# A second layer's in-projection in seven block products, with its weights split in advance

## The chip, the cores and the metric

One of the eight cores of one Trainium2 chip runs the kernel. The metric is the device time of one execution, in microseconds, as the median of repeated runs. The engines work side by side and each takes its instructions in the order of the program: TensorE (PE in the profile, its weight loads PEld), VectorE (DVE), ScalarE (ACT), GpSimd (POOL) and SyncE (SP), which issues nearly all DMAs.

## The reference

Attention inside chunks of 64 tokens, a gated layer, and a second layer with the activation h - tanh(h), for 8 x 576 = 4608 tokens of 512 features:

```
attn = softmax(q k^T / 8) v          per head and chunk of 64
x    = attn, as (4608, 512)
y    = (silu(x @ w_gate) * (x @ w_val)) @ w_out      w_gate, w_val: 512 x 1536
h    = y @ w2_in                                     w2_in: 512 x 2048
out  = (h - tanh(h)) @ w2_out                        w2_out: 2048 x 512
```

All weights come as 64-bit floats.

## The kernel before, in words

**Numbers.** Each float is split into a high and a low half that TensorE reads exactly; a product takes three passes (`PASSES`: high x high, high x low, low x high). Splitting is a cast to the high half (`copy`, L294, ACT) and a subtraction for the low one (`sub`, L252, DVE). A 64-bit weight is first turned into a float by `convert`: a load into a `raw` tile, one ACT instruction (`mag`) and four on DVE.

**Sweeps, blocks, units.** Tokens go in 9 blocks of 512. There are three sweeps over the blocks: sweep 0 and sweep 1 do half each of the gated layer's 1536 hidden features (3 pairs of 256 for each block), sweep 2 the second layer (8 pairs for each block). A *unit* is one block and one pair of two strips of 128 hidden features: 27 + 27 + 72 units. Between sweeps the activations go to DRAM and back (`xd`, `x2p`, `x2d`).

**The gated layer** (sweeps 0 and 1) multiplies in blocks. `x_set` makes four blocks and three sums of blocks of the activations (B11, B21, B22, T1 to T4) and splits them, `cols_set` does so for the weights, and `in_proj` then needs seven products (a to g, `ORDER`) in place of eight, each of 6 matmuls with 256 columns. The products share two PSUM banks, X for a, c, e, g and Y for b, d, f; between them ACT copies a partial sum out (`snap0` to `snap3`) or DVE adds one (L249).

**The second layer** (sweep 2) multiplies directly: `in_whole` makes each strip in four steps (one for each 128 input features) of three matmuls with 512 columns, into a bank for each strip. `cubic_set` computes h - tanh(h) from that bank: ACT makes the square, the tanh and a bracket (`sq`, `th`, `br`), DVE a comparison, h - tanh, a cube, a polynomial and a selection (`gt`, `re`, `cu`, `po`, `se`), then the split (`h`, `l`). All of its weights stay in SBUF.

**Out-projection.** `out_parts` of a unit are eight steps of three matmuls with 512 columns, worked off two units later. After the last pair of a block ACT or DVE copies the finished sums out.

**The order of the work** is written out by hand. `PE` has a letter for each step of a unit (letters or digits for the in-projection, `o` for a step of the out-projection). One letter is one *slot*. The table `AT` gives for every other step the slot after its start at which it is issued, `ON` the engine, `START` the start of each preparation of weights. What is issued on an engine runs in that order there.

**Weights of the second layer before.** During sweep 1 `ahead_set` converts them into a `cvt` tile and stores that to DRAM. `whole_set` loads the floats back around the start of sweep 2 and splits them into tiles that stay.

Of the kernel before, what the change touches and what calls it, by code (L numbers as in the profile page):

```python
# [1257 lines left out]
```

## Time and profile before

| | |
|---|---|
| median of 3 runs | 1842.05 us (1841.13 to 1843.69) |
| span of the profiled execution | 1838.3 us, 3.75 us below the median |
| TensorE busy in the span | 1754.7 us |
| VectorE, ScalarE, GpSimd busy | 1341.1, 923.3, 176.7 us |
| sweep 2's first and last in-projection matmul start | 1020.8 and 1821.8 us |

The profile is of one execution; its own time outside the span is not recorded, so the difference to the median is all that is known of it. Times in the rows are from the span's start. A busy PE says that matmuls follow one another, not at which rate; the rate is read from counts in a window.

### The profile page before, as it was taken

The numbers are of one execution on the slowest core, as the hardware profiler recorded it, in microseconds if no ns is written. First come the engines' busy times: TensorE is split into PE (matmuls) and PEld (weight loads), VectorE is DVE, ScalarE is ACT, GpSimd is POOL, SyncE is SP. The second block draws the span as 40 slices with busy tenths as digits, with TensorE's granted clock in tenths as the row PEclk, the third lists the DMA queues.
The fourth block names the chain that finished last, engine by engine and source line by source line (L and its number), as shares of the span: only waits on it lengthen the run. The fifth ranks groups of instructions, "written<-read, shape, count | busy, mean of one in ns | idle before, by whom it ended". The sixth has DMA issues, their size and how long they took to land.

```text
span 1838.3 us, 30622 instructions
## 1 busy us (share of the span) xinstructions
PE 1754.7 (95%) x11800; PEld 1509.2 (82%) x11800; DVE 1341.1 (73%) x2438; ACT 923.3 (50%) x1772; POOL 176.7 (10%) x251
## 2 busy tenths in 40 slices
PE   4679999999999899999999999999999999999999
PEld 3669888888898899999998888888888888888887
DVE  7897888778767777777755777676676767676765
ACT  4566655665555544444444545444444444444443
POOL 2233333333210000000000000000000000000000
PEclk9799999999999999999999999999999999999999
DMA  7545545555432454444424401010101000000000
GB/s 183 145 108 135 132 117 144 138 129 130 100 98 70 138 172 138 155 145 148 144 75 149 161 12 46 1 47 0 47 3 44 22 25 23 24 23 24 1 23 23
DMA packets 220802, 158.25 MB, mean 86 GB/s; under 512 B 155376, under 2 KB 180848, under 8 KB 218352
## 3 DMA queue, kind: packets, MB, share of 16 engines
q1 hardware_dynamic: 214256, 148.95, 28.1%
q0 software_dynamic: 6400, 7.35, 1.5%
q8 instruction: 92, 1.51, 0.3%
q14 instruction: 54, 0.44, 0.1%
HBM read 105.38 MB, written 50.86 MB: 85 GB/s over the span
## 4 chain that ended last, share of the span: by engine, by line
PE 85%; DVE 9%; DMA 2%; ACT 2%; issue 1%; SPq 0%; POOL 0%; DVEq 0%; ACTq 0%; POOLq 0%
PE acc L1058 35%; PE H L562 22%; PE Xg L508 7%; PE Xv L508 6%; PE Yg L508 6%; PE Yv L508 5%; PE ppt L671 1%; PE po L746 1%; PE sc L735 1%; DVE xb_B L296 1%; DMA f_wi<-cvt_wi 1%; DVE scratch L252 1%; DVE vs L249 0%; DVE mx L644 0%; DVE xb_B L252 0%
## 5 line engine op out<-in xcount | busy, mean ns | idle before, releaser
L562 PE MATMUL H<-xb,wi 128*128 128x512 f32 x1728 | 490.3, 394 | 0.0
L1058 PE MATMUL acc<-wp,h 128*128 128x512 f32 x1728 | 488.3, 394 | 0.0
L562 PEld LDWEIGHTS H<-xb,wi 128*128 128x128 f32 x1728 | 324.5, 188 | 77.0
L1058 PEld LDWEIGHTS acc<-wp,h 128*128 128x128 f32 x1728 | 324.7, 188 | 75.7
L1058 PE MATMUL acc<-h,wo 128*128 128x512 f32 x1296 | 364.0, 397 | 0.5 <-DVE wo L252 0.5
L1058 PEld LDWEIGHTS acc<-h,wo 128*128 128x128 f32 x1296 | 220.3, 189 | 29.2 <-DVE wo L252 1.0
L508 PEld LDWEIGHTS Xg<-xb_T,wg 128*128 128x128 f32 x972 | 138.5, 191 | 18.2 <-ACT s L294 2.5
L508 PE MATMUL Xg<-xb_T,wg 128*128 128x256 f32 x972 | 144.5, 285 | 3.1 <-DVE xb_T L252 1.7
L712 POOL DMA_DIRECT2D vr<-in_v_dram x200 | 115.8, 591 | 201.2 <-PE po L746 197.2
L294 ACT CAST h<-g 128x512 fp32r<-128x512 f32 x72 | 44.7, 620 | 166.3 <-DVE g L973 166.3
L294 ACT CAST h<-vr 128x512 fp32r<-128x512 f32 x72 | 44.7, 620 | 120.3 <-DVE vr L973 118.1
L508 PE MATMUL Yv<-xb_B,wv 128*128 128x256 f32 x648 | 96.4, 284 | 6.4 <-ACT s L294 4.6
L508 PE MATMUL Xv<-xb_T,wv 128*128 128x256 f32 x648 | 97.7, 287 | 4.1 <-ACT s L294 2.6
L252 DVE TENSOR_TENSOR h<-vs,h 128x512 fp32r<-128x512 f32 x108 | 75.0, 694 | 36.5 <-ACT h L294 35.6
L921 ACT ACTIVATE gs<-gs 128x512 f32<-128x512 f32 x108 | 68.4, 633 | 63.4 <-DVE gs L249 63.1
L508 PE MATMUL Yg<-xb_B,wg 128*128 128x256 f32 x648 | 96.2, 284 | 3.2 <-ACT vs L294 3.2
L508 PEld LDWEIGHTS Yg<-xb_B,wg 128*128 128x128 f32 x648 | 89.2, 191 | 8.5 <-ACT vs L294 3.4
L508 PEld LDWEIGHTS Yv<-xb_B,wv 128*128 128x128 f32 x648 | 84.8, 188 | 11.9 <-ACT s L294 8.2
L508 PEld LDWEIGHTS Xv<-xb_T,wv 128*128 128x128 f32 x648 | 84.7, 190 | 5.1 <-ACT s L294 2.8
L294 ACT CAST h<-vs 128x512 fp32r<-128x512 f32 x108 | 67.2, 623 | 42.3 <-DVE vs L255 21.6
L252 DVE TENSOR_TENSOR h<-g,h 128x512 fp32r<-128x512 f32 x72 | 49.9, 693 | 51.2 <-ACT h L294 51.2
L252 DVE TENSOR_TENSOR h<-vr,h 128x512 fp32r<-128x512 f32 x72 | 49.9, 692 | 46.3 <-ACT h L294 46.3
(235 smaller groups left out, 2744.1 us busy)
## 6 DMA issues: line engine op xcount, KB each, us to landing
xd<-xra SPq DMA_DIRECT2D x36, 256.0 KB, 2.9
x2p<-ob SPq DMA_DIRECT2D x36, 256.0 KB, 2.7
xr_xd<-xd SPq DMA_DIRECT2D x9, 1024.0 KB, 5.2
ob<-x2p SPq DMA_DIRECT2D x36, 256.0 KB, 4.4
x2d<-ob SPq DMA_DIRECT2D x36, 256.0 KB, 2.6
xr_x2d<-x2d SPq DMA_DIRECT2D x9, 1024.0 KB, 4.8
out_dram<-ob SPq DMA_DIRECT2D x36, 256.0 KB, 2.0
raw_wi<-in_moe_w_in_dram SPq DMA_DIRECT2D x16, 512.0 KB, 4.8
```

The costliest lines, as they stand in the source:

```text
L252: eng.tensor_tensor(out=out_, in0=a, in1=b, op=ALU.subtract)
L294: eng.copy(out_, in_)
L296: eng.tensor_copy(out_, in_)
L508: nc.tensor.matmul(bank, w[:, wl, kk * 128:(kk + 1) * 128], x[xn][:, xl, kk, :], start=start and n == 0, stop=n == 5, skip_group_check=not ...
L562: nc.tensor.matmul(u["ps"][j], w[:, wl, k * 128:(k + 1) * 128], x[k][:, xl], start=k == 0 and n == 0, stop=k == KC - 1 and n == 2,)
L671: nc.tensor.transpose(pt[:, m, :], z["p"][:, m].rearrange("p e j -> p (e j)"), ident)
L712: nc.gpsimd.dma_start(out=vr[p:p + C, n + skip:n + m:2], in_=chunks[:, skip:m:2],)
L735: nc.tensor.matmul(sc[e ^ c][c * C:(c + 1) * C, m, :], z["qT"][h, cut], z["kT"][h, cut], start=True, stop=True,)
L746: nc.tensor.matmul(po[c][h, m, :], z["vr"][f, 2 * m + c, :], z["pT"][f, m, c * C:(c + 1) * C], start=True, stop=True,)
L921: return lambda: nc.scalar.activation(out=gs[i], in_=gs[i], func=AF.Silu)
L1058: nc.tensor.matmul(u["acc"][d], l, r, start=p0 and i == 0 and n == 0, stop=p1 and i == 1 and n == 2,)
```

## The change

Three things change, all for the second layer.

1. Its in-projection goes through `in_proj`, as the gated layer's does: seven products a to g of 6 matmuls with 256 columns, so `x_set` now also makes the blocks and sums for sweep 2. A unit has 15 slots in place of 16. `cubic_set` reads the strips from SBUF (tiles `gs`), makes the comparison on ACT (a ReLU of the square minus the threshold) and works in place.
2. The weights are converted and split during sweep 1, one pair in each of the first eight blocks (`split_cols`, `split_rows`), and the split tiles are stored to DRAM. The in-weights are loaded once and stay (`fetch_cols`).
3. The out-weights don't stay: `stream` loads a tile of 512 KB for each strip of each unit, three tiles ahead, when the matmuls on an older tile have been issued.

`raw` tiles and split tiles come from the pool `wrp`, which has 10 buffers in place of 8.

```diff
-PE = ["abocdoefoogABCoDEoFGoo", "aAobBocCodDoeEofFogGoo", "0o1o2o3o4o5o6o7o"]
-LAST = "0o1o2o3o4567oooo"
+PE = ["abocdoefoogABCoDEoFGoo", "aAobBocCodDoeEofFogGoo", "aobocodoeofogoo"]
+LAST = "aobocodoeofogoo"
...
-    wrp = ctx.enter_context(tc.tile_pool(name="wrp", bufs=F2 // 2))
+    wrp = ctx.enter_context(tc.tile_pool(name="wrp", bufs=F1 // 2 + 4))
...
+    def split_rows(start, w, f, nm):
+        z = {}
+        step = Steps("dr", start, f"{nm}{f}")
+        convert(step, "", z, 0, f"{nm}{f}", tile_of(w, f, False), False)
+        def tile():
+            z["t"] = wrp.tile([128, 2, DM], F32R, tag="w", name=f"{nm}{f}")
+            return z["t"][:, 0], z["t"][:, 1]
+        def then():
+            nc.sync.dma_start(out=wf[nm, f], in_=z["t"].bitcast(F32))
+            done.add(("wf", nm, f))
+        halves(step, "", tile, lambda: z["c", 0], ["tl"], then)
...
+    def stream(u, i):
+        w = u["w"][i] = wrp.tile([128, 2, DM], F32R, tag="w", name=f"wp{u['nm']}_{i}")
+        nc.sync.dma_start(out=w.bitcast(F32), in_=wf["wp", 2 * u["pr"] + i])
...
+                if sw.kind == 2 and d == KC - 1 and u["next"][i]:
+                    stream(*u["next"][i])
...
             def large(z=z, tl=tl):
-                nc.vector.tensor_scalar(
-                    out=tl("m"), in0=z["u"], scalar1=SMALL * SMALL, scalar2=None, op0=ALU.is_gt
-                )
+                nc.scalar.activation(
+                    out=tl("m"), in_=z["u"], func=AF.Relu, bias=bias[:, 1:2]
+                )
...
+    for pr in range(h2):
+        first = base[n0[1] + h1 * pr]
+        slot = first + START["dc"]
+        sets.append((slot, lambda slot=slot, pr=pr: split_cols(slot, w2_in, pr, "wi")))
...
-                hp_ = in_whole(u, x)
-                pe = [hp_[int(j)] if j != "o" else j for j in form]
-                cubic_set(u, [b + form.index(j) + 1 for j in "37"])
+                odd = u["pr"] % 2
+                piece = dict(zip("abcdefg", in_proj(
+                    si, wcol["i"], u["pr"], x, lazy("gs", odd),
+                    ("a0", "a1") if odd else ("m0", "m1"), "i" + nm, together,
+                )), o="o")
+                cubic_set(u, b)
```

PE in sweep 2, in the first half of a unit before: H is a strip's bank, xb101_0 to xb101_3 the four parts of the activations, acc a sum of the out-projection.

```order
L562 MATMUL H2_6_3_0_16999<-xb101_0_16695,wi3_0_12454 128x512 x3
L1058 MATMUL acc2_6_0_0_16921<-wp1_0_12281,h2_6_1_0_16893 128x512 x3
L562 MATMUL H2_6_3_0_16999<-xb101_1_16702,wi3_0_12454 128x512 x3
L1058 MATMUL acc2_6_0_1_16932<-wp1_0_12281,h2_6_1_0_16893 128x512 x3
L562 MATMUL H2_6_3_0_16999<-xb101_2_16709,wi3_0_12454 128x512 x3
L1058 MATMUL acc2_6_0_2_16942<-wp1_0_12281,h2_6_1_0_16893 128x512 x3
L562 MATMUL H2_6_3_0_16999<-xb101_3_16718,wi3_0_12454 128x512 x3
L1058 MATMUL acc2_6_0_3_16950<-wp1_0_12281,h2_6_1_0_16893 128x512 x3
```

The same place of the change, products a to f of a block's first unit: Xi and Yi are the two banks.

```order
L518 MATMUL Xi2_6_0_18323<-xb101_B11_18199,wi0_0f_12348 128x256 x6
L1032 MATMUL acc2_5_0_0_17648<-wp2_5_6_0_18184,h2_5_6_0_18261 128x512 x3
L518 MATMUL Yi2_6_0_18324<-xb101_B21_18223,wi0_0f_12348 128x256 x6
L1032 MATMUL acc2_5_0_1_17664<-wp2_5_6_0_18184,h2_5_6_0_18261 128x512 x3
L518 MATMUL Xi2_6_0_18323<-xb101_T2_18251,wi0_1f_12452 128x256 x6
L1032 MATMUL acc2_5_0_2_17678<-wp2_5_6_0_18184,h2_5_6_0_18261 128x512 x3
L518 MATMUL Yi2_6_0_18324<-xb101_T1_18254,wi0_2f_12335 128x256 x6
L1032 MATMUL acc2_5_0_3_17691<-wp2_5_6_0_18184,h2_5_6_0_18261 128x512 x3
L518 MATMUL Xi2_6_0_18323<-xb101_T3_18289,wi0_2f_12335 128x256 x6
L1032 MATMUL acc2_5_0_0_17648<-wp2_5_6_1_18259,h2_5_6_1_18279 128x512 x3
L518 MATMUL Yi2_6_0_18324<-xb101_B22_18271,wi0_1f_12452 128x256 x6
```

Before, a strip's bank is filled by four steps and then read; now a bank is read after each product, and the next product on it comes two products, four slots, later.

DVE before, in the last unit of a block, where the next block's activations (xb117) are split:

```order
L252 TENSOR_TENSOR qT2_7_7_18052<-H2_7_7_0_18013,qT2_7_7_18052 128x512
L252 TENSOR_TENSOR xb117_0_18067<-xr_x2d8_114_17550,xb117_0_18067 128x512
L968 SCALAR_TENSOR_TENSOR vr2_7_7_18065<-kT2_7_7_18060,vr2_7_7_18065 128x512
L252 TENSOR_TENSOR xb117_1_18074<-xr_x2d8_114_17550,xb117_1_18074 128x512
L973 COPY_PREDICATED vr2_7_7_18065<-kr2_7_7_18058,qT2_7_7_18052 128x512
L252 TENSOR_TENSOR xb117_2_18081<-xr_x2d8_114_17550,xb117_2_18081 128x512
L952 TENSOR_SCALAR g102_7_7_18099<-g002_7_7_18087 128x512
L252 TENSOR_TENSOR xb117_3_18090<-xr_x2d8_114_17550,xb117_3_18090 128x512
```

DVE after, at the same place, from the first sum of blocks (on xr) past the add after product b (the 128x256 row); two more rows, a polynomial and a sum, stand before the add after product e.

```order
L239 TENSOR_TENSOR xr_x2d8_115_19436<-xr_x2d8_115_19436 128x2x256
L239 TENSOR_TENSOR vr2_7_6_20016<-gs2_7_6_0_19951,vr2_7_6_20016 128x512
L242 TENSOR_TENSOR gs2_7_6_0_19951<-gs2_7_6_0_19951,qr2_7_6_20009 128x512
L239 TENSOR_TENSOR T_xb117__20053<-xr_x2d8_115_19436 128x512
L239 TENSOR_TENSOR xb117_B11_20047<-xr_x2d8_115_19436,xb117_B11_20047 128x512
L236 TENSOR_TENSOR gs2_7_7_0_20067<-Yi2_7_7_20037,s2_7_7_20038 128x256
L239 TENSOR_TENSOR qT2_7_6_20051<-gs2_7_6_1_19993,qT2_7_6_20051 128x512
L242 TENSOR_TENSOR gs2_7_6_1_19993<-gs2_7_6_1_19993,kr2_7_6_20034 128x512
L938 SCALAR_TENSOR_TENSOR gs2_7_6_0_19951<-qr2_7_6_20009,gs2_7_6_0_19951 128x512
L239 TENSOR_TENSOR xb117_B21_20071<-xr_x2d8_115_19436,xb117_B21_20071 128x512
L943 COPY_PREDICATED gs2_7_6_0_19951<-cvt2_7_6_0_20011,vr2_7_6_20016 128x512
```

The adds that free a bank for PE now stand in one queue with the splitting of the next block and with the activation of the unit before.

SP in sweep 2 before issues one load of activations (xr) and four stores for each block:

```order
L1146 DMA xr_x2d3_109_14120<-x2d3_109 128x2048
L1035 DMA out_0_dram<-ob2_1_7_0_14073 128x512
L1035 DMA out_0_dram<-ob2_1_7_1_14074 128x512
L1035 DMA out_0_dram<-ob2_1_7_2_14131 128x512
L1035 DMA out_0_dram<-ob2_1_7_3_14144 128x512
```

After, the loads of out-weights (wp) stand between them, two for each unit, 16 for each block:

```order
L1014 DMA wp2_1_0_0_13810<-split_wp0_129 128x1024
L1014 DMA wp2_1_0_1_13873<-split_wp1_130 128x1024
L1005 DMA out_0_dram<-ob2_0_7_0_13814 128x512
L1136 DMA xr_x2d2_109_13892<-x2d2_109 128x2048
L1005 DMA out_0_dram<-ob2_0_7_1_13815 128x512
L1005 DMA out_0_dram<-ob2_0_7_2_13891 128x512
L1005 DMA out_0_dram<-ob2_0_7_3_13913 128x512
L1014 DMA wp2_1_1_0_13934<-split_wp2_135 128x1024
L1014 DMA wp2_1_1_1_13999<-split_wp3_136 128x1024
```

SP has 16 loads more in each block; the stores and the loads of activations keep their order among themselves.

PE's order in sweeps 0 and 1 is the same before and after; on ACT, DVE and SP, sweep 1 differs by the converting, splitting and storing of the second layer's weights alone.

## Rows read from the trace of the kernel before

**Rows 1.** The page: span, and busy time of each engine with share and instructions.

```profile
span 1838.3 us, 30622 instructions
...
PE 1754.7 (95%) x11800; PEld 1509.2 (82%) x11800; DVE 1341.1 (73%) x2438; ACT 923.3 (50%) x1772; POOL 176.7 (10%) x251
```

**Rows 2.** Busy time by stage: window, its length, engines (instructions), granted clock, DMA share.

```profile
core 0: us, PE busy (x) PEld busy (x) DVE busy (x) ACT busy (x) POOL busy (x), PEclk, DMA share, GB/s
800.00:900.00 100.00, 100.00 (x696) 93.12 (x696) 71.93 (x138) 47.36 (x104) 0.00 (x0) 1.00 0.45 140
1200.00:1300.00 100.00, 100.00 (x433) 80.97 (x432) 69.65 (x113) 45.33 (x80) 0.00 (x0) 1.00 0.09 32
```

**Rows 3.** The same window of sweep 1, instructions of line 508 (256 columns) alone.

```profile
800.00:900.00 100.00, 71.06 (x540) 70.22 (x540) 1.00 0.45 140
```

**Rows 4.** DVE in sweep 2, 1100 to 1700: line, operation, shapes, busy us, mean ns.

```profile
L973 DVE COPY_PREDICATED g<-g,g 128x512 f32<-128x512 uint32 x54 | 40.9, 758 | 1.9
...
L252 DVE TENSOR_TENSOR h<-g,h 128x512 fp32r<-128x512 f32 x54 | 37.4, 693 | 39.6 <-ACT h L294 39.6
...
L968 DVE SCALAR_TENSOR_TENSOR g<-snap,g 128x512 f32<-128x512 f32 x54 | 36.9, 682 | 0.0
...
L252 DVE TENSOR_TENSOR g<-H,g 128x512 f32<-128x512 f32 x54 | 36.8, 681 | 0.0
...
L952 DVE TENSOR_SCALAR kr<-qr 128x512 f32<-128x512 f32 x54 | 23.1, 427 | 43.7 <-ACT qr L946 43.7
```

**Rows 5.** ACT in sweep 2, 1100 to 1700, in the same form.

```profile
L963 ACT ACTIVATE snap<-g,bias 128x512 f32<-128x512 f32 x54 | 39.3, 728 | 0.0
...
L294 ACT CAST h<-vr 128x512 fp32r<-128x512 f32 x54 | 33.5, 620 | 87.6 <-DVE vr L973 87.6
...
L946 ACT ACTIVATE g<-H 128x512 f32<-128x512 f32 x54 | 32.4, 599 | 43.1 <-PE H L562 42.6
...
L294 ACT COPY ob<-acc 128x512 f32<-128x512 f32 x28 | 16.4, 587 | 16.3 <-PE acc L1058 16.3
```

**Rows 6.** DVE and ACT in sweep 1, 700 to 1000.

```profile
L921 ACT ACTIVATE gs<-gs 128x512 f32<-128x512 f32 x38 | 24.0, 633 | 54.4 <-DVE gs L249 54.4
...
L249 DVE TENSOR_TENSOR gs<-Yg,s 128x256 f32<-128x256 f32 x38 | 16.0, 422 | 11.1 <-PE Yg L508 11.1
...
L294 ACT COPY s<-Xg 128x256 f32<-128x256 f32 x38 | 14.1, 372 | 31.2 <-PE Xg L508 31.2
```

**Rows 7.** Timeline, 1209 to 1213: start, duration, instruction.

```profile
1209.70 0.60 ACT L946 ACTIVATE g<-H 128x512 f32<-128x512 f32 x1 [1.05 <-PE H L562]
...
1210.20 0.59 ACT L949 ACTIVATE g<-H 128x512 f32<-128x512 f32 x1
...
1210.82 0.69 DVE L255 TENSOR_TENSOR g<-H,g 128x512 f32<-128x512 f32 x1
...
1211.43 0.68 DVE L252 TENSOR_TENSOR g<-H,g 128x512 f32<-128x512 f32 x1
```

**Rows 8.** PE's waits, 500 to 700 us: total, times, longest.

```profile
PE Xg L508 <- ACT gs L294: 3.1, 2, 2.8
...
PE Yv L508 <- DVE vs L249: 1.5, 1, 1.5
```

**Rows 9.** Timeline of ACT, 640 to 656: one instruction, its idle time before.

```profile
640.67 0.66 ACT L319 ACTIVATE cvt_wi<-raw_wi 128x512 f32<-128x512 f32 x1 [5.32 <-DMA f_wi<-cvt_wi]
```

**Rows 10.** DMA issues: number, KB each, median us to landing.

```profile
xr_x2d<-x2d SPq DMA_DIRECT2D x9, 1024.0 KB, 4.8
out_dram<-ob SPq DMA_DIRECT2D x36, 256.0 KB, 2.0
...
f_wp<-f_wp SPq DMA_DIRECT2D x8, 512.0 KB, 3.7
f_wi<-f_wi SPq DMA_DIRECT2D x8, 512.0 KB, 5.4
```

**Rows 11.** Weight loads in sweep 1, 700 to 1000, of one 256-column form.

```profile
L508 PEld LDWEIGHTS Yg<-xb_B,wg 128*128 128x128 f32 x234 | 33.1, 189 | 3.7
```

More of the change, by code (lines that the diff above doesn't have):

```diff
@@ L179 @@
 }
[L180 to L185 removed]
+TEMPS = (dict(u="qr", t="vr", m="+"), dict(u="kr", t="qT", m="+"))
 @with_exitstack
@@ L453, in tile @@
             def tile():
-                t = z["t", i] = wcp.tile([128, 2, 2, 256], F32R, tag="w", name=f"{nm}{pr}_{i}")
+                t = z["t", i] = pool.tile([128, 2, 2, 256], F32R, tag="w", name=f"{nm}{pr}_{i}")
                 return t[:, :, 0], t[:, :, 1]
-            def then():
-                table[pr, i] = z["t", i]
-            halves(step, i, tile, src, after, then)
+            halves(step, i, tile, src, after, lambda: then(i))
         def lone():
+            if table is None:
+                z["t", 3] = pool.tile([128, 1, 2, 256], F32R, tag="w", name=f"{nm}{pr}_3")
+                return z["t", 3][:, 0, 0], z["t", 3][:, 0, 1]
             if pr not in hold:
@@ L467, in lone, with then @@
             return hold[pr][:, h, 0], hold[pr][:, h, 1]
-        def then():
-            table[pr, 3] = z["t", 3]
+        def then(i):
+            if table is None:
+                nc.sync.dma_start(out=wf[nm, pr, i], in_=z["t", i].bitcast(F32))
+                done.add(("wf", nm, pr, i))
+            else:
+                table[pr, i] = z["t", i]
         def sums(i):
@@ L483, in cols_set @@
         block(0, lambda: c(0), there[:1])
-        halves(step, 3, lone, lambda: c(1)[:, 1], there[1:], then)
+        halves(step, 3, lone, lambda: c(1)[:, 1], there[1:], lambda: then(3))
         step("s0", sums(0), [there[1], "l3"])
@@ L490, in cols_set, with fetch_cols, block, f @@
         block(2, lambda: c(1), ["s1"])
+    def fetch_cols(start, pr, nm, table, pool):
+        step = Steps("fc2", start, f"f{nm}{pr}")
+        def block(i):
+            def f():
+                if i < 3:
+                    t = pool.tile([128, 2, 2, 256], F32R, tag="w", name=f"{nm}{pr}_{i}f")
+                else:
+                    if pr // 2 not in hold2:
+                        hold2[pr // 2] = pool.tile(
+                            [128, 2, 2, 256], F32R, tag="w", name=f"{nm}{pr}_3f"
+                        )
+                    t = hold2[pr // 2][:, pr % 2:pr % 2 + 1]
+                table[pr, i] = t
+                nc.sync.dma_start(out=t.bitcast(F32), in_=wf[nm, pr, i])
+            return f
+        for i in range(4):
+            step(f"ld{i}", block(i))
+    def cols_set(name, start, w, pr, nm, table, second):
+        z = {}
+        step = Steps(name, start, f"{nm}{pr}")
+        there = floats(step, z, w, pr, nm, True)
+        blocks(step, z, pr, nm, there, wcp, table, second)
     ORDER = (
@@ L548, in in_proj @@
         return [go(i) for i in range(7)]
-    def in_whole(u, x):
-        def go(j, k):
-            def g():
-                if k == 0:
-                    u["ps"][j] = ps.tile(
-                        [128, TB], F32, tag=("m0", "m1", "a0", "a1")[2 * (u["pr"] % 2) + j],
-                        name=f"H{u['nm']}_{j}",
-                    )
-                w = wcol["i"][2 * u["pr"] + j]
-                for n, (wl, xl) in enumerate(PASSES):
-                    nc.tensor.matmul(
-                        u["ps"][j], w[:, wl, k * 128:(k + 1) * 128], x[k][:, xl],
-                        start=k == 0 and n == 0, stop=k == KC - 1 and n == 2,
-                    )
-                if k == KC - 1:
-                    done.add(("h" + u["nm"], j))
-            return g
-        return [go(j, k) for j in range(2) for k in range(KC)]
-    def whole_x(name, start, key, source, nm, dst):
-        step = Steps(name, start, (key, "x"))
-        z = {}
-        for k in range(KC):
-            def tile(k=k):
-                t = z[k] = one.tile([128, 2, TB], F32R, tag=f"x{X_WHOLE[k]}", name=f"{nm}{k}")
-                return t[:, 0], t[:, 1]
-            def then(k=k):
-                dst[k] = z[k]
-            halves(step, k, tile, lambda k=k: source()[:, k], [(key, "there")], then)
     def x_set(name, start, key, source, nm, dst):
@@ L929, in gate_set, with cubic_set @@
         hidden(step, u, 1, lambda: vs[1], ["m1"])
-    def cubic_set(u, ends):
-        nm = u["nm"]
+    def cubic_set(u, start):
+        nm, hid = u["nm"], u["gs"]
         for i in range(2):
             z = {}
-            step = Steps("c", ends[i], (nm, i))
-            h = u["ps"]
+            step = Steps(f"c{i}", start, (nm, i))
             def tl(what, i=i, z=z):
                 tag = TEMPS[i][what]
-                z[what] = one.tile([128, TB], F32, tag=tag, name=f"{tag}{nm}")
+                if tag[0] == "+":
+                    z[what] = rawp.tile([128, TB], F32, tag="cvt", name=f"cvt{nm}_{i}")
+                else:
+                    z[what] = one.tile([128, TB], F32, tag=tag, name=f"{tag}{nm}")
@@ L989, in then @@
                 u["h"][i] = z["h"]
-            halves(step, "", tile, lambda z=z: z["c"], ["se"], then)
-    scratch, xrs, hold = {}, {}, {}
-    wcol, wrow = dict(g={}, v={}, i={}), {1: {}, 2: {}}
+            halves(step, "", tile, lambda i=i: hid[i], ["se"], then)
+    scratch, xrs, hold, hold2 = {}, {}, {}, {}
+    wcol, wrow = dict(g={}, v={}, i={}), {1: {}}
     class Sweep:
@@ L1113, in chunk_attention_moe_moe @@
     for n, job in enumerate(todo):
-        m, sweep = (n, 0) if n < START["ah count"] else (n - START["ah count"], 1)
-        slot = base[n0[sweep]] + START[f"ah{sweep}"] + START[f"ah{sweep} every"] * m
+        slot = base[n0[0]] + START["ah0"] + START["ah0 every"] * n
         sets.append((slot, lambda slot=slot, job=job: ahead_set(slot, *job)))
+    for pr in range(h2):
+        first = base[n0[1] + h1 * pr]
+        slot = first + START["dc"]
+        sets.append((slot, lambda slot=slot, pr=pr: split_cols(slot, w2_in, pr, "wi")))
+        for i in range(4):
+            wf["wi", pr, i] = dram.tile(
+                [128, 2 if i < 3 else 1, 2, 256], F32, name=f"split_wi{pr}_{i}"
+            )
+        for i in range(2):
+            f, s = 2 * pr + i, first + START[f"dr{i}"]
+            sets.append((s, lambda s=s, f=f: split_rows(s, w2_out, f, "wp")))
+            wf["wp", f] = dram.tile([128, 2, DM], F32, name=f"split_wp{f}")
     for j, pr in enumerate(sweeps[1].pairs):
@@ L1122, in chunk_attention_moe_moe @@
     for pr in range(h2):
-        for x, w, nm, table in (("c", w2_in, "wi", wcol["i"]), ("r", w2_out, "wp", wrow[2])):
-            slot = base[n0[2]] + START[f"{x}{pr}"]
-            sets.append((slot, lambda slot=slot, w=w, pr=pr, nm=nm, x=x, table=table: whole_set(
-                slot, w, pr, nm, x == "c", table, HOME[f"{x}{pr}"]
-            )))
+        slot, pool = base[n0[2]] + START[f"f2{pr}"], wcp if pr < 6 else wrp
+        sets.append((slot, lambda slot=slot, pr=pr, pool=pool: fetch_cols(
+            slot, pr, "wi", wcol["i"], pool
+        )))
+    parts2 = [(u, i) for u in units[n0[2]:] for i in range(2)]
+    for n, (u, i) in enumerate(parts2):
+        u.setdefault("w", {})
+        u.setdefault("next", {})[i] = parts2[n + 3] if n + 3 < len(parts2) else None
+        if n < 3:
+            issue(base[n0[2]] + START[f"w{n}"], lambda u=u, i=i: stream(u, i))
     sets.sort(key=lambda x: x[0])
```

148 lines of the change are left out of this document (55 added, 93 removed), and 135 rows, old and new, of tables (AT, LAST, ON, START).

## Prediction

> **What bounds the kernel now.** I read the page first: TensorE (PE) is busy 1754.7 of 1838.3 us [rows 1]. The table by stage then shows where it isn't. In the middle of sweep 1 (800 to 900 us) and of sweep 2 (1200 to 1300) PE is busy for the whole 100.0 us, at a granted clock of 1.00, the upper level, while VectorE (DVE) has 71.9 and 69.7 us of work and ScalarE (ACT) 47.4 and 45.3 [rows 2]. So in sweep 2, which runs from 1020 us to the end, the time is the number of matmuls times what one takes; DVE, ACT and the DMA queue are hidden, and matter only where PE would wait for them. The edit cuts PE's work and adds to the other three. So I price the cut, and then look for places where the cover wears through.
>
> **Price of a matmul.** Sweep 2 issues 432 matmuls of 512 columns in 100.0 us (216 at each of two lines, 433 recorded): 231.5 ns each [rows 2]. Sweep 1 mixes them: of 696 in 100.0 us, 540 have 256 columns [rows 3], the other 156 have 512. 156 x 231.5 ns = 36.1 us; the remaining 63.9 us over 540 give 118.3 ns for 256 columns.
>
> **PE's part.** A unit of sweep 2 has 48 matmuls of 512 now: 11.11 us. After, it has 7 products x 6 = 42 of 256 and the same 24 of the out-projection: 42 x 0.1183 + 24 x 0.2315 = 10.53 us. A product slot then takes 0.71 us, an out slot 0.69. The cut is 0.58 us per unit, **-42 us** over 72 units. It counts in full only if nothing else makes PE wait.
>
> **DVE and ACT inside a unit.** DVE loses the comparison (0.43 us, twice) and gains three adds of 256 columns out of PSUM (0.42 us in sweep 1) [rows 4, 6]: 2 x (0.68 + 0.69 + 0.68 + 0.76 + 0.69) + 3 x 0.42 = 8.3 us of 10.53. ACT gains four copies of 256 columns (0.37) and two comparisons, which I price as the bracket (0.73), since both read SBUF with a bias; its two reads of the hidden strip now come from SBUF, for which I take sweep 1's silu (0.63) in place of 0.60 [rows 5, 6]. That is 4 x 0.37 + 2 x (0.63 + 0.63 + 0.73 + 0.73 + 0.62) = 8.2 us. Both fit, so neither binds on average. They can still be late, because products share two PSUM banks: product c overwrites what ACT copies after a, d what DVE adds after b, and so on to g. Between a product and the next writer of its bank stand out, product, out: 0.69 + 0.71 + 0.69 = 2.1 us. At worst a running instruction (0.76) and then the add (0.42), or 0.73 and the copy (0.37), come first: 1.2 us. The hidden strip itself has a unit of slack: its lower half is made some ten slots into the next unit and used a unit after that. I price the steady unit at 0.
>
> **The unit before a new block.** Here the cover is thin. Splitting the next block's activations costs DVE four sums and seven lower halves, 11 x 0.69 = 7.5 us (four instructions before), and ACT seven casts of 0.62, on top of the unit's own work. Take the order of DVE shown above with the change, from the first sum to the add after e: eleven instructions of 0.69, one of 0.76, two of 0.42: 9.1 us. DVE starts on them some 0.9 us early, since a steady unit's last lower half is done by then (estimated by laying the same durations end to end), and is through at 8.2; g, which needs this, starts at 8.4. Thirteen more up to the add after b of the next unit cost 7.8 us and end at 16.0, when product d should have started at 10.53 + 4.21 = 14.7: 1.3 us late. But durations overlap. Independent DVE instructions of 0.69 start 0.60 us after one another, ACT's of 0.60 start 0.50 apart [rows 7]. With 0.08 us less on each of 25 instructions the same add is 0.7 us early. ACT's queue, laid out likewise, misses by 0.4 us at the means and is in time at the start-to-start distances; the four evictions of finished sums (0.59 each [rows 5]) fill a further unit to 10.5 us and could add 0.8. So a boundary costs between 0 and 2.5 us. The row nearest to it is the observed distance, so I take the low side, 0.7 us: 8 boundaries, **+5.5** (0 to 20).
>
> **Weights.** Every out-projection tile, 512 KB, now arrives by DMA in each unit. Three buffers rotate, and the load is issued when the last matmul on the buffer's old tile is through. Its use comes 15 or 16 slots later, some 11 us; such loads land in 3.7 to 5.4 us [rows 10]. The rate is 1.05 MB per 10.5 us, 100 GB/s beside the 32 of sweep 2 now; sweep 1 moved 140 at 45% of the DMA engines' time [rows 2]. Hidden: 0.
>
> **Sweep 1.** The instructions of PE are the same. Per block, DVE gains the splitting (3.5 + 2 lower halves and four short sums, 5.5 us); the conversions, 4 per block, were there at a similar rate. DVE goes from 72% to some 82%, in the order mostly in the first two units, where no activations are split. PE's slack is larger here: between two users of a bank stand five slots, 3.5 us. Writing the split tiles takes 2.9 MB per block of 46 us where storing converted floats takes 1.2, so 140 GB/s become some 175. I take **+2** (0 to 8). In exchange, in the first block PE waited 1.5 us for DVE and 2.8 for ACT, and ACT stood 5.3 us in front of a conversion whose buffer was still being stored to DRAM [rows 8, 9]. The converted floats of the second layer are no longer stored from that buffer, so these waits have no cause left; new tiles share four buffers, which may bring others: **-3** (-4.3 to +1). Entering sweep 2, the first weights come by DMA already split, without casts, but the activations need three more pieces: 0 (-1 to +2). At the very end the last hidden strip is made in a longer chain behind 5.6 us of out-projection: **+0.5**.
>
> **Sum.** -42 + 5.5 + 2 - 3 + 0.5 = -37 us. The span is 1838.3 us and the median of the three runs 1842.05, 3.75 above; I carry that over: 1842 - 37 = **1805 us**.
>
> **Rivals.**
> *Boundaries at full price.* DVE and ACT miss their places at each new block by the full means, and sweep 1 pays too: -42 + 20 + 8 - 3 + 0.5 = -16.5, **1825 us**. For it: DVE's and ACT's shares rise to 80 to 90% in sweep 2, and the queue of each is worked through in its order, urgent adds behind split halves. Against: the start-to-start distances [rows 7], and sweep 1, where boundaries of the same eleven instructions cost PE nothing between 700 and 1000 us (busy 100.0 of 100.0 in the middle [rows 2]).
> *Weight loads bind; slower.* Each matmul has its own weight load, 189 ns in sweep 1 [rows 11]. A unit would have 66 for 48. Were one such duration the least spacing of two loads, the unit would last 66 x 0.189 = 12.5 us for 11.1, +1.4 x 72 = +100 us: **1940 us**, and it decides from a spacing of 10.53 / 66 = 160 ns upwards. Against it: in sweep 1 696 loads fit into 100.0 us, 144 ns apart, and their durations add up to 132 us, so they overlap. The Trainium skill (Perfetto Trace Analysis, Identifying the Most-Contended Engine) tells to judge TensorE's headroom by the busy share of weight loads rather than that of matmuls; by that rule a stage at 93% (sweep 1) has next to none left, and moving sweep 2 from 81% towards it would use up what the shorter matmuls give. The trace here does not bear this out, since the stage at 93% issues matmuls faster.
> *The weight stream is late; slower.* If the queue served one load after the other at the 5.4 us of [rows 10], a block would need 16 x 5.4 + 4.8 + 4 x 2.0 = 99 us for 84 of PE: +15 x 9 = +135, **1940 us**. It decides once a tile holds the queue for over 5.3 us. Against: 140 GB/s at a share of 0.45 [rows 2] is 0.52 MB in 3.7 us at less than half the engines' time, so landing time is latency, not occupancy.
>
> **Chances.** Forecast (about 1794 to 1814): 0.70. Full price or part of it at the boundaries and in sweep 1 (1814 to 1832): 0.20. A mixture of waits in every unit that uses up the gain within 0.2% (3.7 us, about what a measurement of this kernel tells from none): 0.04. Stream or weight loads: 0.04. Better than 1794, since the lowest sum of bounds is -42 - 4.3 - 1: 0.02. So faster 0.92, same 0.04, slower 0.04. The range takes the low bound and most of the first rival: 1794 to 1825.
>
> **What would show it.** Sweep 2 in windows: some 627 matmuls in 100 us (66 per 10.53 us) with PE at 100.0 in the middle of a block means the cut is real; the list of PE's waits with three to eight waits per block on ACT's copies, DVE's adds or the lower halves of xb, all near a new block, gives the boundary price; PE waiting for a DMA of wp shows the stream rival; matmuls of 256 columns further apart than 118 ns without a wait show the loads. In the first block of sweep 1 the long stand of ACT before a conversion should be gone. I am wrong if PE's waits stand in every unit: then the two banks, not the columns, set the pace.

## The result, and the profile after

The changed kernel takes 1791.23 us (median of 4 runs, 1791.07 to 1793.08), the kernel before beside it 1842.87 us (4 runs, 1841.13 to 1844.02): a ratio of 0.9722, 95% interval 0.9708 to 0.9736. The forecast of 1805 us was 13.8 us too high, and the lower end of its range, 1794, lies 2.8 us above the time.

The page of the profile after, first part (compare [rows 1]):

```profile
span 1789.5 us, 34329 instructions
...
PE 1712.4 (96%) x13096; PEld 1545.2 (86%) x13096; DVE 1409.2 (79%) x2622; ACT 1146.6 (64%) x2247; POOL 178.7 (10%) x251
```

The span is 48.8 us shorter, and it is that of a run of 1791.24 us: 1.74 us lie around it. The table by stage, in the form and the windows of [rows 2]:

```profile
800.00:900.00 100.00, 100.00 (x698) 93.22 (x697) 79.33 (x154) 50.84 (x112) 0.00 (x0) 1.00 0.54 182
1200.00:1300.00 100.00, 100.00 (x628) 90.03 (x627) 78.86 (x135) 77.80 (x148) 0.00 (x0) 1.00 0.44 143
```

Sweep 2 has 628 matmuls in 100.0 us where it had 433, and PE still has no gap: 66 of them, a unit, take 10.51 us. DVE went from 69.7 to 78.9 us, ACT from 45.3 to 77.8. Sweep 1 keeps its 696 to 698 matmuls, though DVE has 7 us more in 100. PE's waits after, from 500 to 700 us, the view of [rows 8] (total, times, longest):

```profile
PE Yg L518 <- DVE gs L236: 1.6, 1, 1.6
PE Xg L518 <- DVE vs L236: 1.1, 1, 1.1
PE Xv L518 <- ACT sqr L278: 0.8, 1, 0.8
PE Xv L518 <- ACT vs L278: 0.6, 1, 0.6
PE Yv L518 <- ACT s L278: 0.6, 1, 0.6
```

Five waits and 4.7 us; before they were eight and 8.8 us. All five stand ahead of the last store of x2p (626.4 us), where the kernel before has five of 3.9 us. Behind it PE waited three times before, the 1.5 and 2.8 us of [rows 8] and

```profile
645.96 0.50 PE L1058 MATMUL acc<-h,wo 128*128 128x512 f32 x1 [0.54 <-DVE wo L252]
```

and doesn't wait at all after. From 1000 us to the end the same view has one row, the sum T1 or T2 of sweep 2's first block:

```profile
PE Yi L518 <- DVE xb_T L239: 0.8, 1, 0.8
```

There is no wait at any later block. The view leaves out waits below 0.15 us; by the starts in the trace no later matmul of sweep 2 comes more than 0.12 us late. Where the 48.8 us went is read from three operations that both kernels have: the last store of x2p (end of sweep 0), the first and last store of x2d (the first finished block of sweep 1, and its end), and the last copy of a finished sum. The view by tile gives their first and last start; before:

```profile
L1035 SPq DMA_DIRECT2D x2p<-ob x36: 319/376/1387, 160.8 to 625.5; - x36
L1035 SPq DMA_DIRECT2D x2d<-ob x36: 319/320/320, 666.2 to 1045.0; - x36
L294 ACT COPY ob<-acc x72: 568/587/602, 158.6 to 1834.7; 128x512 f32<-128x512 f32 x72
```

and after:

```profile
L1005 SPq DMA_DIRECT2D x2p<-ob x36: 319/376/432, 161.8 to 626.4; - x36
L1005 SPq DMA_DIRECT2D x2d<-ob x36: 319/320/320, 661.4 to 1038.2; - x36
L278 ACT COPY ob<-acc x72: 566/587/610, 159.6 to 1785.9; 128x512 f32<-128x512 f32 x72
```

The changed kernel is 0.9 us later at the end of sweep 0, 4.8 earlier after the first block of sweep 1 (a gain of 5.7 there), 6.8 earlier at its end (2.0 more), and 48.8 at the end: 42.0 in sweep 2. The last store of x2d lies some two units into sweep 2, so 1.2 of those 2.0 us are the first two units' cut.

### The profile page after: what moved, and what is told of

Its sections match the earlier page's. It is cut to its first block, busy times and chain, and to the rows that moved or that the text cites. A ratio compares the mean times of both kernels' runs of the same rounds, so it can differ in the third digit from the quotient of the medians.

```text
span 1789.5 us, 34329 instructions
## 1 busy us (share of the span) xinstructions
PE 1712.4 (96%) x13096; PEld 1545.2 (86%) x13096; DVE 1409.2 (79%) x2622; ACT 1146.6 (64%) x2247; POOL 178.7 (10%) x251
## 4 chain that ended last, share of the span: by engine, by line
PE 88%; DVE 8%; issue 1%; ACT 1%; DMA 1%; POOL 0%; DVEq 0%; ACTq 0%; POOLq 0%
PE acc L1032 37%; PE Xi L518 11%; PE Yi L518 9%; PE Xg L518 8%; PE Xv L518 7%; PE Yg L518 6%; PE Yv L518 5%; PE ppt L640 1%; PE po L715 1%; PE sc L704 1%; DVE xb_B L280 1%; DVE scratch L239 1%; DVE vs L236 0%; DVE h L239 0%; DVE sm L622 0%
## 5 line engine op out<-in xcount | busy, mean ns | idle before, releaser
L1032 PE MATMUL acc<-wp,h 128*128 128x512 f32 x1728 | 479.9, 394 | 0.0
L1032 PEld LDWEIGHTS acc<-wp,h 128*128 128x128 f32 x1728 | 291.6, 188 | 33.2 <-DVE h L239 0.3
L278 ACT CAST h<-gs 128x512 fp32r<-128x512 f32 x144 | 89.6, 622 | 86.5 <-DVE gs L943 84.3
L236 DVE TENSOR_TENSOR gs<-Yi,s 128x256 f32<-128x256 f32 x144 | 60.8, 423 | 65.0 <-PE Yi L518 59.7
L239 DVE TENSOR_TENSOR vr<-gs,vr 128x512 f32<-128x512 f32 x72 | 49.8, 692 | 54.7 <-ACT vr L919 54.7
L239 DVE TENSOR_TENSOR h<-gs,h 128x512 fp32r<-128x512 f32 x144 | 92.6, 684 | 0.2 <-ACT h L278 0.2
L242 DVE TENSOR_TENSOR vs<-vs,gs 128x512 f32<-128x512 f32 x108 | 75.3, 697 | 8.1 <-ACT gs L890 5.3
L278 ACT COPY s<-Xg 128x256 f32<-128x256 f32 x108 | 40.1, 371 | 57.2 <-PE Xg L518 54.8
```

The source lines that it names most:

```text
L236: eng.tensor_tensor(out=out_, in0=a, in1=b, op=ALU.add)
L239: eng.tensor_tensor(out=out_, in0=a, in1=b, op=ALU.subtract)
L242: eng.tensor_tensor(out=out_, in0=a, in1=b, op=ALU.mult)
L278: eng.copy(out_, in_)
L1032: nc.tensor.matmul(u["acc"][d], l, r, start=p0 and i == 0 and n == 0, stop=p1 and i == 1 and n == 2,)
```

## The experiments

Twelve kernels ran. The changed kernel ran again with some of them, and its eight runs have a median of 1791.27 us (1789.73 to 1793.85), from which the last column is counted. The ratio is to the kernel before in the same batch of runs.

Medians of one kernel differ by some 2 us from batch to batch. In the traces this scatter stands before the end of sweep 0: the last store of x2p starts between 624.7 and 628.9 us in the changed kernel and its variants, which do the same work up to there. From sweep 2's first in-projection matmul to the last copy of a finished sum the changed kernel took 772.5 us and, run again, 772.6. So for an edit in sweep 2 the text also says by how much this stretch is longer than 772.5 us ("in the stretch").

| kernel | median (range, runs) | ratio, 95% | to the changed kernel |
|---|---|---|---|
| changed kernel again | 1792.33 (1789.73 to 1793.85, 4) | 0.9733, 0.9720 to 0.9746 | +1.1 |
| six more matmuls a unit | 1842.73 (1840.97 to 1844.96, 10) | 1.0009, 0.9999 to 1.0019 | +51.5 |
| one more on DVE, sweep 2 | 1796.59 (1795.53 to 1798.73, 4) | 0.9759, 0.9746 to 0.9773 | +5.3 |
| four more on DVE, sweep 2 | 1814.26 (1812.98 to 1814.40, 4) | 0.9854, 0.9839 to 0.9869 | +23.0 |
| four more on ACT, sweep 2 | 1803.85 (1803.38 to 1804.87, 4) | 0.9798, 0.9785 to 0.9811 | +12.6 |
| comparison on DVE | 1804.06 (1803.26 to 1804.34, 4) | 0.9789, 0.9776 to 0.9803 | +12.8 |
| four more on DVE, sweep 1 | 1793.58 (1792.45 to 1795.22, 4) | 0.9740, 0.9725 to 0.9754 | +2.3 |
| eight more on DVE, sweep 1 | 1819.28 (1818.34 to 1820.97, 4) | 0.9881, 0.9865 to 0.9898 | +28.0 |
| before, conversions later | 1835.99 (1834.16 to 1836.60, 7) | 0.9968, 0.9958 to 0.9979 | |
| splitting later | 1791.32 (1789.06 to 1792.72, 5) | 0.9729, 0.9715 to 0.9742 | 0.0 |
| every tile moved twice | 1794.80 (1792.66 to 1796.51, 4) | 0.9749, 0.9735 to 0.9764 | +3.5 |
| loads two tiles ahead | 1805.10 (1803.87 to 1807.32, 5) | 0.9795, 0.9782 to 0.9809 | +13.8 |

### The changed kernel again

> The changed kernel itself once more, beside the kernel before. Theory on the step from span to time (the time of a run is its own span and about 1.75 us, and the 3.75 us carried in the prediction compared a profiled execution with other, longer ones): each run 1.7 to 1.8 us above its own span; median 1789.5 to 1792. Rival (the median stands 3.75 us above the span): about 1793.

Its four runs stand 1.73 to 1.79 us above their own spans (1788.0 to 1792.1), though their median is 0.3 us over the expected 1792. The step is settled: what lies around a span is 1.7 to 1.8 us here and at most 2.0 in any run, and the 3.75 of the prediction held 2 us that belong to the choice of the run.

### Six more matmuls in each unit

```diff
                 product(Y if i in (1, 3, 5) else X, table, pr, x, i)
+                if i == 0 and si == 2:
+                    product(X, table, pr, x, i)
```

> The changed kernel with the first product of each unit of sweep 2 issued twice: six more matmuls of 256 columns in each of the 72 units. Theory (PE alone sets sweep 2 and a matmul of 256 columns costs 118.3 ns): 72 x 6 x 0.1183 = +51 us, 1842 us, with PE busy for 100.0 us in 100. Rival (ACT and DVE hold the banks back in every unit by waits that the trace does not name, so that more PE work is partly free): under +40 us.

+51.5 us for 72 x 6 matmuls is 119 ns each, and +50.9 in the stretch is 118, against the 118.3 of the prediction. A window of sweep 2:

```profile
1300.00:1400.00 100.00, 100.00 (x641) 90.73 (x640) 74.19 (x127) 73.91 (x140) 0.00 (x0) 1.00 0.40 128
```

PE stays at 100.0 with the extra work: nothing else was setting the pace, and the cut in columns accounts for sweep 2's gain.

### More work at a block boundary of sweep 2

Four kernels add work to DVE or ACT there. The first two repeat a lower half of the sum T2, once or four times, the third its high half:

```diff
             def then(xn=xn):
                 dst[xn] = z["t", xn]
+                if xn == "T2" and key[0] == 2 and key[1]:
+                    for _ in range(4):
+                        t = z["t", xn]
+                        lower(t[:, 1], block(xn), t[:, 0], nc.vector)
```

```diff
                 t = z["t", xn] = one.tile([128, 2, 2, HB], F32R, tag=f"x{xn}", name=f"{nm}{xn}")
+                if xn == "T2" and key[0] == 2 and key[1]:
+                    for _ in range(4):
+                        copy(nc.scalar, t[:, 0], block(xn))
```

> The changed kernel with four more lower halves of 128x512 on DVE (repeats of one that is there) at each of the eight block boundaries of sweep 2. Theory (the start-to-start distance of 0.60 us is what an instruction costs DVE's queue, and at a boundary the add after b is about 0.1 us ahead of product d, so the cover is used up): 4 x 0.60 - 0.1 = 2.3 us a boundary, 18 us in all, about 1809 us. Rival one (durations of 0.69 count in full): 4 x 0.69 - 0.1 = 2.7, 21 us. Rival two (there is slack of more than 2.4 us somewhere and the boundary is free with a wide margin): no difference, 1791 us.

> The changed kernel with one more lower half of 128x512 on DVE at each of the eight block boundaries of sweep 2; four of them cost 2.7 us a boundary by the spans, where each took 0.72 us of DVE's queue. Theory (the cover at a boundary is used up to about 0.15 us, so the very first added instruction is paid for): 8 x (0.72 - 0.15) = 4.5 us, about 1796. Rival (there is a threshold of 1 us or more, and the four cost so much because a late PE makes other engines late in turn): 0 to 1 us, 1791.

> The changed kernel with four more casts of 128x512 on ACT (repeats of the high half of the same sum) at each of the eight block boundaries of sweep 2. ACT stands for 0.88 us behind them, and its copy after product a was 0.16 us ahead of product c. Theory (ACT's cover is as thin as DVE's): 4 x 0.52 to 4 x 0.62 less 1.04 is 1.0 to 1.4 us a boundary, 8 to 12 us in all, 1799 to 1803. Rival (DVE alone is tight, and ACT, which often stands behind DVE, takes them in): within 1 us of the changed kernel.

First the place itself, in the changed kernel. The timeline of each engine around the first product (1436.34) of a new block:

```profile
1435.35 0.43 DVE L236 TENSOR_TENSOR gs<-Yi,s 128x256 f32<-128x256 f32 x1
1435.68 1.29 DVE L239 TENSOR_TENSOR h<-gs,h 128x512 fp32r<-128x512 f32 x2
...
1439.42 0.69 DVE L242 TENSOR_TENSOR gs<-gs,qr 128x512 f32<-128x512 f32 x1
1440.03 0.42 DVE L236 TENSOR_TENSOR gs<-Yi,s 128x256 f32<-128x256 f32 x1
```

```profile
1438.65 0.35 ACT L278 COPY s<-Xi 128x256 f32<-128x256 f32 x1
```

```profile
1438.46 0.87 PE L1032 MATMUL acc<-wp,h 128*128 128x512 f32 x3
1439.16 0.89 PE L518 MATMUL Xi<-xb_T,wi_1f 128*128 128x256 f32 x6
1439.89 0.86 PE L1032 MATMUL acc<-wp,h 128*128 128x512 f32 x3
1440.58 0.66 PE L518 MATMUL Yi<-xb_T,wi_2f 128*128 128x256 f32 x4
```

ACT's copy after a ends at 1439.00 and c starts at 1439.16; DVE's add after b ends at 1440.45 and d starts at 1440.58. Both starts are on time, 0.70 us after the step before. So the adds and copies that the prediction named arrive, with 0.13 and 0.16 us to spare.

The runs show that this really is all. One added instruction on DVE costs 5.3 us (4.3 against the changed kernel of the same batch, 4.7 in the stretch): 0.6 a boundary of its 0.72, as the theory had it. PE's waits then name ACT's copy after a, not DVE's add:

```profile
PE Xi L518 <- ACT s L278: 1.6, 8, 0.4
```

In ACT's timeline at one boundary the first read of the finished strip waits 0.58 us for DVE's last add to it, and the copy stands five instructions behind that read. Four more cost 23.0 us (22.5 in the stretch), 2.8 a boundary. DVE's timeline with four more:

```profile
1445.30 3.60 DVE L239 TENSOR_TENSOR xb_T<-T_xb__17297,xb_T 128x512 fp32r<-128x512 f32 x5
1448.82 0.42 DVE L236 TENSOR_TENSOR gs<-Yi,s 128x256 f32<-128x256 f32 x1
```

Five in a row up to the next start take 3.52 us, 0.70 each, where independent ones start 0.60 apart [rows 7], so the expectation of 18 us used too small a step, and the rival of 21 us was nearer by its size. And the wait stands elsewhere, as PE's timeline shows:

```profile
1447.61 0.63 PE L1036 MATMUL acc<-wp,h 128*128 128x512 f32 x2
1449.89 0.50 PE L1036 MATMUL acc<-wp,h 128*128 128x512 f32 x1 [1.65 <-DVE h L239]
...
1452.47 0.99 PE L518 MATMUL Xi<-xb_T,wi_1f 128*128 128x256 f32 x6 [0.68 <-ACT s L278]
```

The lower half of a hidden strip, behind the split halves in DVE's queue, is late first (1.65 us), then ACT's copy (0.68), which in turn had been waiting for DVE. The queue's delay is paid once, at whatever PE meets first.

Four casts on ACT cost 12.6 us (11.5 in the batch, 12.4 in the stretch), at the top of or just above the 8 to 12 of the theory, and PE's waits in sweep 2 name ACT alone:

```profile
PE Xi L518 <- ACT s L278: 10.3, 8, 1.3
```

The rival, that ACT has room because it often stands behind DVE, falls.

The fourth puts the comparison back on DVE:

```diff
-                nc.scalar.activation(
-                    out=tl("m"), in_=z["u"], func=AF.Relu, bias=bias[:, 1:2]
+                nc.vector.tensor_scalar(
+                    out=tl("m"), in0=z["u"], scalar1=SMALL * SMALL, scalar2=None, op0=ALU.is_gt
                 )
```

> The changed kernel with the comparison made on DVE again (an is_gt on the square, 0.43 us, twice a unit) in place of ACT's ReLU. Theory (a steady unit has room, a boundary has none: three units around a boundary keep DVE busy without a gap, with 0.35 us of queue for each comparison): 2 to 4 comparisons count at each of eight boundaries, 0.7 to 1.4 us each, less nothing: 5 to 11 us, 1797 to 1803, and no wait in the middle of a block. Rival (ACT is relieved by as much, and ACT was as tight as DVE, so that the two cancel): within 2 us of the changed kernel.

+12.8 us, 11.5 of them in the stretch, just above the 5 to 11 expected. Of sweep 2's waits:

```profile
PE Yi L518 <- DVE gs L236: 8.8, 9, 1.1
```

Nine waits, one of 0.34 us in the first block and eight of 1.05, all before product d near a block's start, and none in the middle. The place was right. The size was somewhat low: each wait named costs PE some 0.3 us more than its length (see the last section). So the part of the change that moves the comparison to ACT is worth some 11.5 us, nearly all at block boundaries.

### The same in sweep 1

The edit is that of the lower halves with `key[0] == 1`, four and eight times.

> The changed kernel with four more lower halves of 128x512 on DVE (2.9 us of its queue at 0.72 each) at each of eight block boundaries of sweep 1, where the next block's activations are split as in sweep 2. Theory (between two products on one bank stand 3.5 us of other steps in sweep 1, against 2.1 in sweep 2, so the added work of the change had room there): within 2 us of the changed kernel, 1790 to 1794. Rival (DVE at 79% is as tight there as in sweep 2): 8 x 2.7 = 22 us, 1813.

> The same with eight (5.8 us of DVE's queue at each boundary of sweep 1). Theory (3.5 us of room): at most 5.8 - 3.5 = 2.3 us a boundary, 18 us, 1792 to 1810. Rival (tight from the first instruction on): 8 x 5.7 = 46 us, 1837.

Four more (2.9 us) bring one wait of PE, at the first of the eight boundaries (638.9 us), in the view of 500 to 700 us:

```profile
PE Xg L518 <- DVE gs L236: 1.1, 1, 1.1
```

The other seven boundaries show none. The median moves by 2.3 us; the first block of sweep 1, from the last store of x2p to the first of x2d, is 1.8 us longer (36.8 for 35.1), the rest of sweep 1 is not. So the theory held at seven boundaries and missed the first. With eight, PE's waits from 690 us on begin with this row:

```profile
PE Xg L518 <- DVE gs L236: 12.6, 7, 1.8
```

Seven boundaries wait 1.8 us each, and the first, in the first block, 3.9. With 0.3 us for each restart the seven lose 2.1 us, near the 5.8 - 3.5 = 2.3 of the theory: sweep 1 has some 3.7 us of cover there, and at its first boundary 1.6 (5.8 - 4.2; with four, 2.9 - 1.4 = 1.5), where sweep 2 has 0.15. Yet the kernel lost 28 us, not 18, because of the first boundary and, above all, TensorE's clock (last section).

### The first block of sweep 1

In the kernel before, the second layer's conversions start later:

```diff
-    "wv2": 77, "wo2": 88, "ah0": 61, "ah0 every": 22, "ah1": 8, "ah1 every": 14,
+    "wv2": 77, "wo2": 88, "ah0": 61, "ah0 every": 22, "ah1": 54, "ah1 every": 14,
```

> The kernel before, with the conversions of the second layer's weights started 46 slots later in sweep 1, behind its first block. Theory (the waits of the first block of sweep 1 came from the second layer's conversions and their stores, and the change removed them): PE's waits between 580 and 670 us fall from 8.8 us to about 4 or 5 and the time falls by 4 to 6 us against the kernel before, to about 1838. Rival (those waits belong to the turn from sweep 0 to sweep 1 and the change shortened the block in another way): no difference, within 1 us of the kernel before.

-5.3 us (1835.99 against 1841.30, 16 runs), and these waits of PE are left between 500 and 700 us:

```profile
PE Xv L508 <- ACT sqr L294: 1.6, 1, 1.6
PE Xg L508 <- DVE vs L249: 0.9, 1, 0.9
PE Yv L508 <- ACT s L294: 0.6, 1, 0.6
PE Yg L508 <- DVE gs L249: 0.5, 1, 0.5
```

None of the three waits behind the last store of x2p is left, as after the change, and ACT starts its conversions there without a wait in both kernels. From that store to the first one of x2d pass 35.1 us in both, against 40.6 before. So the change's gain in this block comes from ridding it of the waits on the conversions, and the kernel before could have had it by one number. The changed kernel with its splitting one block later asks for the rest:

```diff
-        first = base[n0[1] + h1 * pr]
+        first = base[n0[1] + h1 * (pr + 1)]
```

> The changed kernel with the splitting of the second layer's weights started one block later in sweep 1, so that its first block has none of it. Theory (PE's 4.7 us of waits between 580 and 670 us come mostly from the turn of the sweeps, since the kernel before with late conversions still had 3.6 us of them): about 1 us less, 1790. Rival (the splitting itself makes those waits): 3 to 4.7 us less, 1787.

1.0 us less than the changed kernel in the same batch, which these runs can't tell from none; its first block takes 35.1 us as before the edit, and the remaining 3.7 us of waits, there without any splitting, belong to the turn of the sweeps. No version came out clearly below the changed kernel.

### The stream of out-weights

```diff
         nc.sync.dma_start(out=w.bitcast(F32), in_=wf["wp", 2 * u["pr"] + i])
+        nc.sync.dma_start(out=spare[u["pr"] % 4, i], in_=wf["wp", 2 * u["pr"] + i])
```

> The changed kernel with every out-weight tile of sweep 2 also copied from DRAM to a spare place in DRAM behind its load, on the same queue: 144 more transfers of 512 KB. Theory (the landing time of 3.6 us is latency and the queue is less than half used): within 2 us of the changed kernel, 1790 to 1793. Rival (transfers of the queue are served one after another, so that 3.6 us is what each takes of 5.3): 4 x 3.6 = 14.4 us of queue for each unit of 10.5, at least +3.9 x 72 = +280 us, and PE waits for wp.

```profile
1300.00:1400.00 100.00, 99.46 (x622) 89.19 (x621) 78.34 (x133) 76.84 (x145) 0.00 (x0) 1.00 0.63 221
```

221 GB/s at a share of 0.63, and the loads still land after 3.6 us in the median; no wait of PE names wp. The 3.5 us more are over the 2 expected; 2.7 of them stand in the stretch, and 1.4 are three waits for ACT. The rival would have cost 280.

```diff
-        u.setdefault("next", {})[i] = parts2[n + 3] if n + 3 < len(parts2) else None
-        if n < 3:
+        u.setdefault("next", {})[i] = parts2[n + 2] if n + 2 < len(parts2) else None
+        if n < 2:
```

> The changed kernel with the out-weights loaded two tiles ahead in place of three, so that a tile has some 5.6 us between its issue and its first use in place of 11. Theory (a load lands 3.6 us after its issue and the queue is free): within 2 us of the changed kernel, 1790 to 1794, and no wait of PE for wp. Rival (landing times scatter past 5.6 us when the activations' 1 MB or a block's stores stand in the same queue): a wait of 1 to 3 us at each of the blocks, 1800 to 1820.

+13.8 us, 11.9 of them in the stretch: the theory fell. PE waits in sweep 2 seven times for a tile:

```profile
PE acc L1032 <- DMA wp<-split_wp: 10.0, 7, 1.9
```

The issues on SP at one of these places, and, in the second fence, at a like place of the changed kernel:

```profile
1205.68 0.34 SPq L1005 DMA_DIRECT2D out_dram<-ob  x1
1206.07 0.43 SPq L1136 DMA_DIRECT2D xr_x2d<-x2d  x1
1208.19 2.16 SPq L1005 DMA_DIRECT2D out_dram<-ob  x3
1210.45 1.94 SPq L1014 DMA_DIRECT2D wp<-split_wp  x2
```

```profile
1452.79 0.32 SPq L1014 DMA_DIRECT2D wp<-split_wp  x1
1454.81 0.34 SPq L1005 DMA_DIRECT2D out_dram<-ob  x1
...
1457.33 2.16 SPq L1005 DMA_DIRECT2D out_dram<-ob  x3
1459.59 4.07 SPq L1014 DMA_DIRECT2D wp<-split_wp  x2
```

A load is issued when the last user of its buffer is through, and three buffers rotate in both kernels. What the edit moved is the load's place in SP's queue. In the changed kernel one load leaves at 1452.79, 2 us ahead of a block's first store. With two ahead that load stands behind all four stores, which wait for ACT to copy the finished sums; its buffer was free at about 1203.6, the end of the last matmuls on it in PE's timeline, and it left at 1210.45, 4.3 us ahead of its use. It also lands late there, behind the stores and the 1 MB load; the view of this one load gives

```profile
DMA to landing us min/median/max: 5.5/5.5/5.5
```

though the median of all 144 is 3.6 as in the changed kernel. At all seven places the load leaves 4.3 us ahead of its use and lands 5.5 to 6.3 us after it left. So the rival had the landing time and the loss right; what it didn't have is that the order on SP also takes the lead, from 5.6 us to 4.3. With the lead from a free buffer, or with the median landing time, the tile at 1215.98 would have been in time (due at 1214.71).

## Why the prediction was right or wrong

**PE's part: right.** The unit was forecast at 10.53 us and measured 10.51. 72 times the difference to 11.11 is 43 us; sweep 2 gave 42.0 behind the last store of x2d and 1.2 ahead of it. The experiment with six more matmuls confirms price and bound.

**Boundaries: the term that failed.** The step reads "I take the low side, 0.7 us: 8 boundaries, +5.5". Measured is 0: no wait at any of the eight. The prediction's own laying-out at the observed distances had the add 0.7 us early and ACT in time; the trace has both in time by 0.13 and 0.16. (Its sums there are 0.1 us low: 11 x 0.69 is 7.6, and the fourteen instructions take 9.2.) The 0.7 was charged in the face of that row, and the 0.8 us of evictions beside it don't meet the boundary: the copies of finished sums start at 1454.20 us, 18 us behind the new block's first product at 1436.34, and ACT idles 1.06 us before the first of them. That the cover is thin was right, as the first added instruction shows, and the rival at full price was near: one instruction of 0.72 us more on DVE at each boundary begins to pay it.

**Sweep 1: sized wrong.** "+2 (0 to 8)" measured 0. Its cover with the added work is still some 3.7 us at seven boundaries and 1.6 at the first.

**First block: sized wrong, right cause.** "-3 (-4.3 to +1)" measured -5.7. The bound was made of two named waits, 1.5 and 2.8 us [rows 8]. The block had a third wait, of 0.5 us, and each wait costs PE some 0.3 us more than its length: 4.9 + 3 x 0.3 = 5.8 us, and all of it went.

**Entry and tail.** Forecast 0 and +0.5. Three waits of before from 690 us on, 1.7 us together, gave way to the one of 0.8: about -0.9. At the end nothing was lost.

**From the span to the median: 2 us.** The profiled execution of before, by the 1.7 to 2.0 us that lie around the span in every run, took about 1840 us. It was shorter than the three runs whose median is 1842.05. Its span should have been set beside a span of the change, and the scatter of some 2 us kept in the range.

**Sum.** Over the spans -5.5 (boundaries), -2 (sweep 1), -2.7 (first block), -0.9 (entry), -0.5 (tail), about -1.2 (a shorter unit and rounding), +0.9 (before sweep 1): -11.9, against the 11.8 us between -37 and -48.8. With the 2 us of the last step that is the 13.8. The range had the boundaries at 0 too; its lowest sum gives 1794.7, and the time lies 3.5 us below that by the other terms: 2.0 (span to median), 1.4 (first block beyond its bound) and 1.2 (unit), less 0.9 (before sweep 1) and 0.1 (entry).

**The slower rivals fell.** Weight loads: in the changed kernel 627 of them fit into 100.0 us, 159 ns apart, and PE is never idle. The Trainium skill (Perfetto Trace Analysis, Identifying the Most-Contended Engine), which judges TensorE's headroom by MFU and the busy share of weight loads, would by the second have warned of the rise in sweep 2; the share did rise, from 81.0 to 90.0%, and the sweep became shorter by the whole cut. Weight stream: at twice the traffic the median landing time was the same.

## What to carry to other kernels

When the bounding engine loses work, lay the others' queues out at the distances between starts that the trace shows, for the worst unit and not the mean, and keep to the result: here it was right to 0.6 us and a charge on top was the error. Then ask how much is left, since an average share of 79% hid a boundary with 0.15 us to spare in one sweep and 3.7 in another. A load placed behind stores in a DMA-issuing queue leaves later than its buffer allows and lands later than the median: both have to fit into its lead.

## What the runs showed of the hardware

**A stall costs more than the wait that the view names.** With four more on DVE the waits named in sweep 2 beyond the changed kernel's are 17.0 us, the stretch 22.5 longer: 0.3 us for each of 16 waits. With four more on ACT it is 10.3 of 12.4 in 8 waits. About half of this is the view's way of counting: a matmul of 512 columns is recorded with 0.39 us and the next would have started 0.23 after its start, so a wait counted from the record's end is some 0.17 us short. In the timeline above the matmul at 1449.89 would have been due at 1448.07 (231 ns after each of two): 1.82 us late for a wait of 1.65, and the product behind a wait takes 0.99 us where its neighbours take 0.86 to 0.89.

**The clock can fall behind a short stall.** With eight more on DVE in sweep 1, PE stood still at eight boundaries. The table in steps of 1 us behind one of them (the clock is the third number from the end):

```profile
789.00:790.00 1.00, 0.00 (x0) 0.00 (x0) 0.97 (x3) 0.00 (x0) 0.00 (x0) 1.00 0.00 0
790.00:791.00 1.00, 0.86 (x6) 0.78 (x6) 1.00 (x4) 0.00 (x0) 0.00 (x0) 1.00 0.00 0
791.00:792.00 1.00, 1.00 (x7) 0.93 (x6) 1.00 (x4) 0.62 (x2) 0.00 (x0) 0.66 0.00 0
792.00:793.00 1.00, 1.00 (x5) 0.90 (x5) 0.90 (x3) 0.79 (x3) 0.00 (x0) 0.50 0.00 0
793.00:794.00 1.00, 1.00 (x3) 0.77 (x3) 0.68 (x2) 0.14 (x1) 0.00 (x0) 0.50 0.03 8
794.00:795.00 1.00, 1.00 (x5) 0.80 (x4) 0.48 (x1) 1.00 (x3) 0.00 (x0) 0.64 0.00 0
795.00:796.00 1.00, 1.00 (x10) 1.00 (x10) 0.89 (x3) 1.00 (x3) 0.00 (x0) 1.00 0.00 0
```

PE stood for 1.80 us up to 790.14; 1.2 us after it had started again the granted clock went to 0.50, the level of 1.2 GHz, and came back at about 794.7. That costs 0.34 + 0.50 + 0.50 + 0.36 = 1.7 us. It happened at five of the eight boundaries, and not at 840 us behind a wait of the same 1.80 us. Waits 16.6, restarts 8 x 0.3 and five falls 8.5 make 27.5 us, against the 27.2 by which the span grew (28.6 from the end of sweep 0 to sweep 2's first matmul). In sweep 2 the waits of 1.65 and 0.68 us at one boundary brought no fall. Nor does the wait's length alone decide: a wait of 1.6 us at the turn to sweep 1 (597 to 601 us) stands in every trace of the changed kernel and its variants with the splitting in its place, and in two of them (six more matmuls, comparison on DVE) the clock is 0.50 at 602 us, in the others 1.00. What decides was not tried.

**Repeats on one tile went slower through DVE.** 0.70 to 0.72 us from start to start for lower halves written to the same tile, 0.60 for those to different ones, at the same duration of 0.69.
